# One replayed order for all engines behind attention in a retention, Mish and GLU kernel

## The chip, the cores and the metric

The kernel runs on one core of a Trainium2 chip. The metric is the device time of one execution in microseconds (us); lower is better. Engines are TensorE (PE; its weight loads are PEld), VectorE (DVE), ScalarE (ACT), GpSimd (POOL) and SyncE (SP), whose queue issues the transfers.

## The reference

Linear attention with a decaying state, then two feed-forward layers. Sizes: 2 batches, 8 heads, 768 positions, head width 64, so 1536 tokens by 512 features; inner widths 2048 and 1536; all float32.

```python
for t in range(S):
    state = gamma * state + outer(k[t], v[t])
    y[t] = scale * q[t] @ state
x = y as [1536, 512]
h = x @ moe_w_in                       # 512 x 2048
x = (h * tanh(softplus(h))) @ moe_w_out
gate = sigmoid(x @ moe2_w_gate)        # 512 x 1536
out = (gate * (x @ moe2_w_val)) @ moe2_w_out
```

## The kernel before, in words

**Precision.** Each float32 operand is kept as a rounded part (hi) and a remainder (lo). A product is three matmuls, hi·hi, hi·lo and lo·hi (mm3). So each weight and each activation needs a copy on ScalarE (hi) and a subtraction on DVE or GpSimd (lo); this pair is split, lines 94 to 96.

**Weights** come as 68 pieces of 512 KB. SP loads a piece into one of two staging buffers (raw), ScalarE and DVE decode it in two steps each (lines 106 to 109), and put (lines 192 to 200) writes hi and lo into a ring: 7 buffers "w", 4 "o", 2 "q". The kernel looks ahead: after each step of products, pump plans and emits the next weight as far as a ring has room.

**Products.** The 1536 tokens are 3 chunks of 512. From the third pair of blocks of the inner width on (and in the second layer), seven products replace eight (a Strassen-Winograd form): chunks 1 and 2 make the main product (512 columns, banks "h"), and the two halves of chunk 0 the side product (256 columns, banks "hx"). This needs sums of the inputs: main_sums forms T1 to T4 from chunks 1 and 2, side_sums the same (tiles ty, YT, and T4 in a part of xc) from the halves of chunk 0; sums (lines 202 to 211) does it for the weights on GpSimd. out1 and out2 are the second products of the two layers; each bank "o" is evicted into acc by ScalarE (first time, lines 467 and 481) or added by DVE (lines 469 and 483).

**Order.** While attention runs (the flag early is set), all five engines are bound to the written order through InOrder. The side sums are written into attention's blocks, two steps per block. Behind attention only TensorE keeps the written order; the framework's own scheduler orders the other engines at build time from its timeline simulation, within a priority for the second main sums (line 712). Every engine still runs its queue strictly in that fixed order on the chip. Which engine forms a remainder is written out: blocks and main sums on DVE, side sums and remainders of g on GpSimd, of weights on DVE and, from line 698 on, on GpSimd.

Of the kernel before, what the change touches and what calls it, by code (L numbers as in the profile page):

```python
# [9 lines left out]
F32 = mybir.dt.float32  # L10
F32R = mybir.dt.float32r
# [12 lines left out]
def kernel(ctx, tc, qk, nv, w1i, w1o, w2g, w2v, w2o, ma_in, og_in, sg_in, ck_in, out):  # L24
# [26 lines left out]
    AHEAD = 4  # L51

    early = [True]

    class InOrder:


        def __init__(self, engine):
            self.engine, self.last = engine, None

        def __getattr__(self, name):
            call = getattr(self.engine, name)
            if not early and self.engine is not nc.tensor:
                return call

            def ordered(**kw):
                with tc.issue_after(self.last) if self.last else nullcontext():
                    i = call(**kw)  # L68
                self.last = i.ins
                return i  # L70

            return ordered

    pe, dve, act, pool, sync = [InOrder(e) for e in (nc.tensor, nc.vector, nc.scalar, nc.gpsimd, nc.sync)]
    const = ctx.enter_context(tc.tile_pool(name="const", bufs=1))
    big = ctx.enter_context(tc.tile_pool(name="big", bufs=1))
    rings = {r: ctx.enter_context(tc.tile_pool(name="ring_" + r, bufs=RINGS[r])) for r in "wo"}
    upv = ctx.enter_context(tc.tile_pool(name="upv", bufs=3))
    stg = ctx.enter_context(tc.tile_pool(name="stg", bufs=STG))
    dec = ctx.enter_context(tc.tile_pool(name="dec", bufs=3))  # L80
    gp = ctx.enter_context(tc.tile_pool(name="gp", bufs=8))
    ep = ctx.enter_context(tc.tile_pool(name="ep", bufs=3))
    ps_h = ctx.enter_context(tc.tile_pool(name="ps_h", bufs=4, space=PSUM))
    ps_o = ctx.enter_context(tc.tile_pool(name="ps_o", bufs=2, space=PSUM))

    one_t = const.tile([P, 1], F32, name="one")
    sig = const.tile([P, 1], F32, name="sig")
# [53 lines left out]
    lo_eng = {"w": dve, "g": pool}  # L141

    def load_piece():
        n = cnt["dma"]
# [57 lines left out]
    def sums(key):  # L202
        v1, v2 = vs.pop(key)
        s = lo_eng["dcs"].tile([P, 4, H], F32, tag="s", name="s")
        a11, a12, a21, a22 = v1[:, :H], v1[:, H:], v2[:, :H], v2[:, H:]
        tt = pool.tensor_tensor
        tt(out=s[:, 0], in0=a21, in1=a22, op=ALU.add)
        tt(out=s[:, 1], in0=s[:, 0], in1=a11, op=ALU.subtract)
        tt(out=s[:, 2], in0=a11, in1=a21, op=ALU.subtract)
        tt(out=s[:, 3], in0=a12, in1=s[:, 1], op=ALU.subtract)  # L210
        sums_t[key] = s
# [56 lines left out]

    def put_plain():
        for kk in range(KK):  # L270
            split(acc_t[0][:, kk], xc_t[:, kk, 0], xc_t[:, kk, 1], dve)

    def put_block(n, c, k0, eng=None):
        for k in range(2):
            split(acc_t[c][:, k0 + k], b_t[n][:, k, 0], b_t[n][:, k, 1], eng or dve)

    def put_sums(x0, x1, bt, cols, eng):

        def new(n):
            return (up if cols == N else upv).tile([P, cols], F32, tag="u", name=n)  # L280

        sub = eng.tensor_tensor
        ts = []
        for k in range(2):
            t1, t2 = new("t1"), new("t2")
            sub(out=t1, in0=x1[:, k], in1=x0[:, k], op=ALU.subtract)
            split(t1, bt["T1"][:, k, 0], bt["T1"][:, k, 1], eng)
            sub(out=t2, in0=x1[:, 2 + k], in1=t1, op=ALU.subtract)
            split(t2, bt["T2"][:, k, 0], bt["T2"][:, k, 1], eng)
            sub(out=t2, in0=x0[:, 2 + k], in1=t2, op=ALU.subtract)  # L290
            ts.append(t2)
            sub(out=t1, in0=x1[:, 2 + k], in1=x1[:, k], op=ALU.subtract)
            split(t1, bt["T3"][:, k, 0], bt["T3"][:, k, 1], eng)
        return ts

    def put_t4(ts, bt, eng):
        for k in range(2):
            split(ts[k], bt["T4"][:, k, 0], bt["T4"][:, k, 1], eng)

    def main_sums():  # L300
        return put_sums(acc_t[1], acc_t[2], b_t, N, dve)

    def side_sums():

        x0, x1 = acc_t[0][:, :, :H], acc_t[0][:, :, H:]
        t = {}

        def form(n, k, in0, in1, to=None):
            if to is None:
                to = upv.tile([P, H], F32, tag="u", name="ty")  # L310
            pool.tensor_tensor(out=to, in0=in0, in1=in1, op=ALU.subtract)  # L311
            t[n, k] = to
            if n != "T4":
                low(n, k)

        def low(n, k):
            split(t[n, k], y_t[n][:, k, 0], y_t[n][:, k, 1], pool)

        steps = []
        for k in range(2):  # L320
            steps += [lambda k=k: form("T1", k, x1[:, k], x0[:, k]),
                      lambda k=k: form("T2", k, x1[:, 2 + k], t["T1", k]),
                      lambda k=k: form("T4", k, x0[:, 2 + k], t["T2", k], t["T2", k]),
                      lambda k=k: form("T3", k, x1[:, 2 + k], x1[:, k], t["T1", k])]
        return steps + [lambda k=k: low("T4", k) for k in range(2)]


    g_t = {}
# [159 lines left out]
    def seq(ss):  # L488

        def step(f):  # L490
            f()
            if not early:
                pump()

        return [lambda f=f: step(f) for f in ss]

# [55 lines left out]
    with ExitStack() as actx:  # L552
# [82 lines left out]
            at_state(j)  # L635
            at_out(j)

        ys = side_sums()

        def blocks(j0, dense, made):  # L640

            for j in range(j0, j0 + SPC):
                if j + 1 < NSUB:
                    at_scores(j + 1)
                if j >= SPC - 1:
                    pump()
                fin(j)
                flush_hi()
                at_prep(j + 2)
                load(j + AHEAD)  # L650
                load_piece()
                if j == j0 + SPC - 1:
                    flush()
                    made()
                if dense:
                    dense.pop(0)()
                if j >= SPC + 1:
                    run(ys[:2])
                    del ys[:2]
            run(dense)  # L660

        for t, table in ((ck, ck_in), (ma, ma_in), (og0, og_in), (sg, sg_in)):
# [12 lines left out]
        at_scores(0)  # L675
        blocks(0, [], put_plain)
        blocks(SPC, plain1(0) + plain1(1), lambda: (put_block("B11", 1, 0), put_block("B21", 1, 2)))
        blocks(2 * SPC, plain1(0, 1) + plain1(1, 1), early.clear)

    big2 = ctx.enter_context(tc.tile_pool(name="big2", bufs=1))  # L680
    up = ctx.enter_context(tc.tile_pool(name="up", bufs=3))
    dcs = ctx.enter_context(tc.tile_pool(name="dcs", bufs=1))
    rings["q"] = ctx.enter_context(tc.tile_pool(name="ring_q", bufs=RINGS["q"]))
    ps_x = ctx.enter_context(tc.tile_pool(name="ps_x", bufs=1, space=PSUM))
    hx["pool"], hx["own"] = ps_x, (0, 1)
    lo_eng["dcs"] = dcs
# [12 lines left out]
    L1 = FF1 // 2 - 1  # L699
    rest = out1(0, 2, G0)  # L700
    for i in range(I0, L1 + 1):
# [14 lines left out]
    run(ys[:8], plain2(1), ys[8:])  # L716
# [69 lines left out]
```

## Time and profile before

| | |
|---|---|
| median of 3 runs | 630.2 us (628.78 to 632.59) |
| profiled execution, its time | 630.01 us |
| its span | 628.2 us |
| TensorE, DVE, GpSimd, ScalarE busy | 591.5, 409.1, 346.5, 291.3 us |
| mean granted TensorE clock | 0.978 of full |

Attention takes roughly the first 82 us of the span, the first layer lies between 82 and 338, the second behind that. Times in rows are counted from the span's start. A matmul's record is longer than the step from one start to the next, because products overlap in the engine; 512-column products follow each other at some 0.23 us.

### The profile page before, as it was taken

What the parts mean: (1) busy time and instruction counts of PE and PEld (TensorE: products, weight loads), DVE (VectorE), ACT (ScalarE), POOL (GpSimd) and SP (SyncE); (2) the same over time, 40 slices, a digit from 0 to 9 for tenths busy, and PEclk for the clock granted to TensorE, in tenths of its full rate; (3) what the DMA queues carried; (4) which work ended last, traced back from release to release, by engine and by line L of the source; (5) the groups of instructions that cost most, each with busy time, mean ns of one, the idle gap of its engine ahead of it and who ended that gap; (6) DMA issues with size and microseconds to landing.
All of it is one profiled execution on the core that took longest, in us unless ns stands there. A gap on an engine that the chain in (4) does not pass through costs nothing.

```text
span 628.2 us, 8737 instructions
## 1 busy us (share of the span) xinstructions
PE 591.5 (94%) x3342; PEld 492.6 (78%) x3342; DVE 409.1 (65%) x585; ACT 291.3 (46%) x533; POOL 346.5 (55%) x299
## 2 busy tenths in 40 slices
PE   8987969799899999999979998989999999999997
PEld 7875858688688888888847777868888888888886
DVE  3875879606757575756798576538668767754564
ACT  1445575527436353536665575534534544440220
POOL 4476743308948484529893698637746745751200
PEclk9989898899899999999999999989999999999999
DMA  9962233202303131303130042203104104000004
GB/s 348 379 231 106 70 99 100 67 1 83 119 35 100 34 100 35 101 0 102 64 105 1 1 134 72 96 2 127 42 34 134 38 31 135 1 1 0 1 22 179
DMA packets 15593, 52.30 MB, mean 83 GB/s; under 512 B 1984, under 2 KB 2112, under 8 KB 15552
## 3 DMA queue, kind: packets, MB, share of 16 engines
q1 hardware_dynamic: 14976, 51.39, 23.4%
q8 instruction: 26, 0.43, 0.3%
q10 hardware_dynamic: 576, 0.36, 0.2%
q14 instruction: 15, 0.12, 0.1%
HBM read 48.60 MB, written 3.15 MB: 82 GB/s over the span
## 4 chain that ended last, share of the span: by engine, by line
PE 60%; DVE 14%; POOL 10%; ACT 7%; DMA 6%; issue 3%; SPq 0%; DVEq 0%; ACTq 0%; POOLq 0%
PE o L68 28%; PE h L68 20%; PE hx L68 11%; DVE v L109 3%; DMA raw<-w1i 2%; POOL ww L198 2%; DVE T L96 2%; POOL g L96 2%; DVE v L68 1%; DMA raw<-w2v 1%; DVE raw L108 1%; DVE raw L68 1%; DMA qk_t<-qk 1%; POOL ty L311 1%; POOL g L68 1%
## 5 line engine op out<-in xcount | busy, mean ns | idle before, releaser
L68 PE MATMUL o<-g,wo 128*128 128x512 f32 x576 | 147.3, 405 | 17.3 <-ACT acc L467 7.3
L96 POOL TENSOR_TENSOR g<-e,g 128x512 fp32r<-128x512 f32 x74 | 105.2, 1427 | 79.8 <-ACT g L95 75.3
L68 PEld LDWEIGHTS o<-g,wo 128*128 128x128 f32 x576 | 109.0, 195 | 44.1 <-ACT acc L467 8.2
L68 PE MATMUL o<-wo,g 128*128 128x512 f32 x432 | 110.0, 395 | 0.3 <-POOL g L96 0.3
L68 PE MATMUL h<-B,ww 128*128 128x512 f32 x372 | 95.6, 394 | 0.0
L68 PE MATMUL h<-T,ww 128*128 128x512 f32 x360 | 91.9, 392 | 2.7 <-DVE e L454 1.0
L68 PEld LDWEIGHTS o<-wo,g 128*128 128x128 f32 x432 | 78.7, 190 | 15.3 <-POOL g L96 0.7
L198 POOL TENSOR_TENSOR ww<-s,ww 128x512 fp32r<-128x512 f32 x32 | 43.1, 1352 | 80.3 <-ACT ww L197 74.9
L68 PEld LDWEIGHTS h<-T,ww 128*128 128x128 f32 x360 | 67.4, 189 | 17.9 <-DVE e L454 1.5
L68 PEld LDWEIGHTS h<-B,ww 128*128 128x128 f32 x372 | 69.6, 190 | 15.0 <-issue 0.5
L106 ACT ACTIVATE raw<-raw 128x512 int32<-128x512 uint8 x59 | 39.7, 672 | 86.6 <-DMA raw<-w1o 18.7
L108 DVE SCALAR_TENSOR_TENSOR raw<-raw 128x512 int32<-128x512 int32 x59 | 56.0, 948 | 34.3 <-ACT raw L106 33.8
L469 DVE TENSOR_TENSOR acc<-o,acc 128x512 f32<-128x512 f32 x72 | 48.8, 686 | 32.3 <-PE o L68 32.3
L109 DVE SCALAR_TENSOR_TENSOR v<-v,raw 128x512 int32<-128x512 int32 x59 | 60.9, 1032 | 13.9 <-ACT v L107 12.8
L483 DVE TENSOR_TENSOR acc<-o,acc 128x512 f32<-128x512 f32 x60 | 41.3, 688 | 31.0 <-PE o L68 30.9
L95 ACT ACTIVATE g<-e 128x512 fp32r<-128x512 f32 x77 | 48.4, 628 | 16.6 <-DVE e L454 16.0
L68 PE MATMUL hx<-xc,ww 128*128 128x256 f32 (+1 forms) x336 | 54.1, 299 | 0.3 <-DVE xc L68 0.3
L68 PEld LDWEIGHTS hx<-xc,ww 128*128 128x128 f32 x336 | 48.8, 190 | 5.2 <-DVE xc L68 0.7
L68 PEld LDWEIGHTS hx<-YT,ww 128*128 128x128 f32 x288 | 40.7, 190 | 8.6 <-DVE u L363 5.0
L68 PE MATMUL hx<-YT,ww 128*128 128x256 f32 x288 | 42.4, 283 | 3.8 <-DVE u L363 3.8
L198 POOL TENSOR_TENSOR wo<-v,wo 128x512 fp32r<-128x512 f32 x24 | 33.4, 1395 | 22.5 <-ACT wo L197 22.5
L107 ACT ACTIVATE v<-raw 128x512 f32<-128x512 f32 x59 | 39.4, 668 | 12.6 <-POOL s L210 5.7
(106 smaller groups left out, 786.9 us busy)
## 6 DMA issues: line engine op xcount, KB each, us to landing
raw<-w1i SPq DMA_DIRECT2D x16, 512.0 KB, 3.3
raw<-w1o SPq DMA_DIRECT2D x16, 512.0 KB, 3.3
qk_t<-qk SPq DMA_DIRECT2D x12, 512.0 KB, 6.0
nv_t<-nv SPq DMA_DIRECT2D x12, 512.0 KB, 6.9
raw<-w2g SPq DMA_DIRECT2D x12, 512.0 KB, 3.4
raw<-w2v SPq DMA_DIRECT2D x12, 512.0 KB, 3.3
raw<-w2o SPq DMA_DIRECT2D x12, 512.0 KB, 3.3
out<-acc SPq DMA_DIRECT2D x12, 256.0 KB, 2.0
```

The lines of the kernel that those rows point to most:

```text
L68: i = call(**kw)
L95: act.activation(out=hi, in_=raw, func=AF.Copy)
L96: eng.tensor_tensor(out=lo, in0=raw, in1=hi.bitcast(F32), op=ALU.subtract)
L106: act.activation(out=low, in_=rest, func=AF.Copy, scale=1.0 / 32, bias=-15.5 / 32)
L107: act.activation(out=v, in_=high.bitcast(F32), func=AF.Copy, scale=2.0 ** -112)
L108: dve.scalar_tensor_tensor(out=low, in0=high, scalar=SIGN, in1=low, op0=ALU.bitwise_and, op1=ALU.bitwise_or)
L109: dve.scalar_tensor_tensor(out=b, in0=b, scalar=3, in1=low, op0=ALU.logical_shift_left, op1=ALU.bitwise_or)
L198: late_lo.append(lambda: lo_eng["w"].tensor_tensor(out=lo, in0=v, in1=hi.bitcast(F32), op=ALU.subtract))
L311: pool.tensor_tensor(out=to, in0=in0, in1=in1, op=ALU.subtract)
L469: dve.tensor_tensor(out=acc, in0=o, in1=acc, op=ALU.add)
L483: dve.tensor_tensor(out=acc, in0=o, in1=acc, op=ALU.add)
```

## The change

Attention itself is written as before, in order, but the side sums are no longer in its blocks, and the flag early is cleared after attention's last products. From there on no call issues an instruction. Each call makes a Node with its engine (or two: "either" means GpSimd or DVE), its price, and the nodes that it must follow, from the words of the tiles that it reads and writes and from the buffers that it reuses. TensorE's nodes form a chain in written order. At the end replay() gives every node a rank, the price of the longest chain from it to the end, plays all nodes through on a clock, and issues them in the order of their planned starts, each behind the one before it on its engine. A free engine takes the ready node with the highest rank, but not one that would keep a single-engine node of higher rank waiting past its latest start. DVE takes an "either" node only if GpSimd could not start it by its latest start.

"Either" are now: remainders of weights, of g and of blocks, the steps of main and side sums, and the sums of weights. The steps of main and side sums are cut the same way (sums_of). pump is called with 12 instead of 1 (while recording), the priority of line 712 and the late assignments to DVE or GpSimd go.

```diff
-    pe, dve, act, pool, sync = [InOrder(e) for e in (nc.tensor, nc.vector, nc.scalar, nc.gpsimd, nc.sync)]
+    class Node:
+        def __init__(self, queues, name, kw):
...
+            self.cost = [q.cost(big.at.size, kw) for q in queues]
+            self.uses = [(v.home, k == "out", v.words()) for k, v in parts]
...
+            for home, writes, words in self.uses:
+                for n, w, m in home.uses:
+                    if (w or writes) and m & words:
+                        self.after.add(n)
...
+    pe = Queue(nc.tensor, lambda n, kw: (kw["rhs"].at.size + 32) / 2400, 0.2)
+    dve = Queue(nc.vector, lambda n, kw: (0.157 + 0.00104 * n) * (1 if psum(kw) else 1.3), 0.1)
+    act = Queue(nc.scalar, lambda n, kw: 0.17 + 0.0009 * min(n, N), 0.1)
+    pool = Queue(nc.gpsimd, lambda n, kw: 0.08 + 0.00258 * n, 0.1)
+    sync = Queue(nc.sync, lambda n, kw: 3.3 if isinstance(kw["out"], Part) else 1.6, 0.3)
+    either = Either(pool, dve)
...
+        for n in order:
+            n.rank = n.cost[0] + max((lag(n, m) + m.rank for m in n.then), default=0)
+        whole = max(n.rank for n in nodes)
...
+                for n in sorted((n for n in line[q] if n.ready <= now), key=lambda n: -n.rank):
+                    cost = n.cost[n.queues.index(q)]
+                    if len(n.queues) > 1 and q is dve:
+                        if max(now, free[pool]) + n.cost[0] <= whole + late - n.rank + n.cost[0]:
+                            continue
+                    end = now + cost
+                    if any(u.rank > n.rank and u.ready < end and end > max(u.ready, whole + late - u.rank)
+                           and u.ready > now and len(u.queues) == 1 for u in line[q]):
+                        continue
+                    pick = n
+                    break
...
+                late = max(late, n.start - (whole - n.rank)) if q is pe else late
...
+        for n in sorted(nodes, key=lambda n: (n.start, n.at)):
+            n.queue.issue(n.name, n.kw)
...
-        tt = pool.tensor_tensor
+        tt = either.tensor_tensor
...
-                pump()
+                pump(12)
...
-        ys = side_sums()
-
         def blocks(j0, dense, made):
...
-                if j >= SPC + 1:
-                    run(ys[:2])
-                    del ys[:2]
...
-        blocks(2 * SPC, plain1(0, 1) + plain1(1, 1), early.clear)
+        blocks(2 * SPC, plain1(0, 1) + plain1(1, 1), lambda: None)
+        flush()
+    early.clear()
...
+    lo_eng.update(dcs=Pool(name="dcs", bufs=1), w=either, g=either, x=either)
...
-    run(out1(0, 0, G0))
+    run(side_sums(), out1(0, 0, G0))
     ts = main_sums()
-    run(plain1(0, 2), plain1(1, 2))
+    run(ts[:6], plain1(0, 2), plain1(1, 2))
     b_t["T4"] = big2.tile([P, 2, 2, N], F32R, tag="T4", name="T4")
-    run(out1(0, 1, G0))
-    put_t4(ts, b_t, dve)
-    lo_eng["w"] = pool
+    run(ts[6:], out1(0, 1, G0))
...
-    with tc.high_priority():
-        put_t4(main_sums(), b_t, dve)
-        put_block("B22", 2, 2)
+    run(main_sums())
+    put_block("B22", 2, 2)
...
-            lo_eng["g"] = dve
             n = 3
...
+    replay()
```

## Rows read from the trace of the kernel before

**Rows 1.** The page's first part: busy us, share of the span, count.
```profile
PE 591.5 (94%) x3342; PEld 492.6 (78%) x3342; DVE 409.1 (65%) x585; ACT 291.3 (46%) x533; POOL 346.5 (55%) x299
```
**Rows 2.** Busy time by stage: stretch, its length, engines, clock, DMA share, GB/s.
```profile
24.00:82.00 58.00, 51.26 (x498) 40.92 (x497) 40.74 (x51) 27.47 (x54) 35.82 (x34) 0.91 0.45 163
82.00:121.00 39.00, 30.68 (x121) 24.12 (x120) 36.91 (x45) 27.73 (x53) 18.61 (x15) 0.91 0.30 95
121.00:142.00 21.00, 20.89 (x90) 17.30 (x91) 1.18 (x2) 4.52 (x9) 0.93 (x1) 0.92 0.00 1
142.00:163.00 21.00, 18.00 (x87) 14.67 (x86) 12.40 (x17) 17.04 (x32) 18.61 (x15) 0.93 0.31 101
163.00:313.00 150.00, 150.00 (x759) 127.94 (x758) 99.48 (x146) 73.28 (x133) 94.37 (x79) 1.00 0.19 64
313.00:386.00 73.00, 64.10 (x276) 49.33 (x275) 58.35 (x79) 44.05 (x79) 55.41 (x46) 1.00 0.21 71
386.00:420.00 34.00, 30.93 (x156) 26.10 (x155) 13.95 (x24) 14.94 (x28) 16.79 (x17) 0.95 0.14 47
420.00:604.00 184.00, 183.29 (x968) 157.42 (x967) 120.88 (x188) 74.03 (x135) 94.63 (x82) 1.00 0.14 46
```
**Rows 3.** The same view of the windows in which the granted clock was low.
```profile
44.00:47.40 3.40, 3.40 (x32) 2.76 (x28) 3.18 (x5) 1.74 (x3) 2.41 (x3) 0.50 0.41 154
61.00:67.90 6.90, 5.08 (x49) 4.46 (x50) 5.49 (x6) 3.46 (x7) 5.10 (x5) 0.51 0.21 76
91.80:98.60 6.80, 5.69 (x13) 4.46 (x14) 6.80 (x11) 4.28 (x10) 1.66 (x2) 0.50 0.01 2
122.50:125.90 3.40, 3.40 (x10) 2.63 (x9) 0.00 (x0) 0.40 (x1) 0.00 (x0) 0.50 0.00 0
```
**Rows 4.** TensorE's waits: us in total, times, the longest.
```profile
PE st L68 <- POOL YT L68: 5.6, 2, 3.6
PE o L68 <- POOL g L96: 4.5, 4, 2.4
PE o L68 <- DVE acc L469: 4.5, 5, 1.4
```
**Rows 5.** GpSimd in order of time in attention: start, us, instruction, idle before.
```profile
58.23 0.72 POOL L68 TENSOR_TENSOR ty<-acc 128x256 f32<-128x256 f32 x1
...
62.10 1.49 POOL L68 TENSOR_TENSOR vp<-nv_t,ck 128x512 f32<-128x512 f32 x1
```
**Rows 6.** The side sums' steps in attention by tile: count, ns min/median/max, first and last start.
```profile
L68 POOL TENSOR_TENSOR YT<-ty,YT x6: 722/730/743, 40.0 to 69.4; 128x256 fp32r<-128x256 f32 x6
L68 POOL TENSOR_TENSOR ty<-acc x4: 722/736/739, 38.7 to 68.2; 128x256 f32<-128x256 f32 x4
L68 POOL TENSOR_TENSOR ty<-acc,ty x4: 722/726/740, 40.7 to 67.5; 128x256 f32<-128x256 f32 x4
...
L68 POOL TENSOR_TENSOR xc<-ty,xc x2: 1177/1219/1261, 75.6 to 76.8; 128x256 fp32r<-128x256 f32 x2
```
**Rows 7.** ScalarE in order of time before 122.
```profile
119.40 0.66 ACT L106 ACTIVATE raw<-raw 128x512 int32<-128x512 uint8 x1 [2.22 <-DMA raw<-w1o]
...
120.49 1.06 ACT L467 ACTIVATE acc<-o 128x512 f32<-128x512 f32 x2
```
**Rows 8.** DVE in order of time before TensorE's start at 411.5.
```profile
410.40 0.69 DVE L108 SCALAR_TENSOR_TENSOR raw<-raw 128x512 int32<-128x512 int32 x1 [1.59 <-ACT raw L106]
411.01 0.41 DVE L363 TENSOR_TENSOR u<-hx,s 128x256 f32<-128x256 f32 x1
```
**Rows 9.** Remainders: tile T on DVE (82 to 121), then GpSimd in order of time.
```profile
L96 DVE TENSOR_TENSOR T<-t,T x8: 677/680/1782, 94.9 to 117.2; 128x512 fp32r<-128x512 f32 x8
...
153.20 1.31 POOL L198 TENSOR_TENSOR ww<-s,ww 128x512 fp32r<-128x512 f32 x1
154.46 1.74 POOL L96 TENSOR_TENSOR g<-e,g 128x512 fp32r<-128x512 f32 x1
```
**Rows 10.** The chain that ended last, its longest piece: start, us, what.
```profile
603.67 20.61 PE o L68 x90
```

More of the change, by code (lines that the diff above doesn't have):

```diff
@@ L53 @@
     early = [True]
-    class InOrder:
-        def __init__(self, engine):
-            self.engine, self.last = engine, None
-        def __getattr__(self, name):
[L62 to L72, printed above, removed]
@@ L74 @@
-    pe, dve, act, pool, sync = [InOrder(e) for e in (nc.tensor, nc.vector, nc.scalar, nc.gpsimd, nc.sync)]
-    const = ctx.enter_context(tc.tile_pool(name="const", bufs=1))
[L76 to L84, printed above, removed]
+    WIDTH = {F32: 4, F32R: 4, I32: 4, I64: 8, U8: 1}
+    nodes = []
+    class Home:
+        def __init__(self, make, before, psum):
+            self.make, self.before, self.psum = make, before, psum
+            self.real, self.uses = make() if early else None, []
@@ new lines, with __init__, __getitem__, bitcast @@
+    class Part:
+        def __init__(self, home, at, width, ops):
+            self.home, self.at, self.width, self.ops = home, at, width, ops
+        def __getitem__(self, key):
+            return Part(self.home, self.at[key[1:]], self.width, self.ops + (lambda t: t[key],))
+        def bitcast(self, dtype):
+            w = WIDTH[dtype]
+            at = (self.at[..., None] + np.arange(self.width // w) * w).reshape(*self.at.shape[:-1], -1)
+            return Part(self.home, at, w, self.ops + (lambda t: t.bitcast(dtype),))
+        def rearrange(self, form, **kw):
+            at = self.at.reshape(-1, kw["t"]) if kw else self.at.reshape(-1)
+            return Part(self.home, at, self.width, self.ops + (lambda t: t.rearrange(form, **kw),))
+        def words(self):
+            m = np.zeros((1 + int(self.at.max()) // 4 + 1), bool)
+            m[self.at.ravel() // 4] = True
+            if self.width == 8:
+                m[self.at.ravel() // 4 + 1] = True
+            return int.from_bytes(np.packbits(m, bitorder="little").tobytes(), "little")
+        def real(self):
+            if self.home.real is None:
+                self.home.real = self.home.make()
+            t = self.home.real
+            for f in self.ops:
+                t = f(t)
+            return t
@@ new lines, with __init__, tile @@
+    class Pool:
+        def __init__(self, bufs, **kw):
+            self.pool, self.bufs, self.psum = ctx.enter_context(tc.tile_pool(bufs=bufs, **kw)), bufs, "space" in kw
+            self.made = {}
+        def tile(self, shape, dtype, name, tag=None):
+            made = self.made.setdefault(tag or name, [])
+            kw = {"tag": tag} if tag else {}
+            before = made[-self.bufs] if len(made) >= self.bufs else None
+            made.append(Home(lambda: self.pool.tile(shape, dtype, name=name, **kw), before, self.psum))
+            at = np.arange(int(np.prod(shape[1:]))).reshape(shape[1:]) * WIDTH[dtype]
+            return Part(made[-1], at, WIDTH[dtype], ())
@@ new lines @@
+    class Node:
+        def __init__(self, queues, name, kw):
+            self.queues, self.name, self.kw = queues, name, kw
+            parts = [(k, v) for k, v in kw.items() if isinstance(v, Part)]
+            big = max((v for _, v in parts), key=lambda v: v.at.size)
+            self.cost = [q.cost(big.at.size, kw) for q in queues]
+            self.uses = [(v.home, k == "out", v.words()) for k, v in parts]
+            if name == "matmul" and not kw["start"]:
+                self.uses.append((kw["out"].home, False, self.uses[0][2]))
+            self.after, self.then = set(), []
+            for home, writes, words in self.uses:
+                for n, w, m in home.uses:
+                    if (w or writes) and m & words:
+                        self.after.add(n)
+            for home, writes, words in self.uses:
+                home.uses.append((self, writes, words))
+            self.at = len(nodes)
+            nodes.append(self)
@@ new lines, with __init__, issue @@
+    class Queue:
+        def __init__(self, engine, cost, lag):
+            self.engine, self.cost, self.lag, self.last = engine, cost, lag, None
+        def issue(self, name, kw):
+            call = getattr(self.engine, name)
+            kw = {k: v.real() if isinstance(v, Part) else v for k, v in kw.items()}
+            with tc.issue_after(self.last) if self.last else nullcontext():
+                i = call(**kw)
+            self.last = i.ins
+        def __getattr__(self, name):
+            return lambda **kw: self.issue(name, kw) if early else Node([self], name, kw)
@@ new lines, with __init__, __getattr__, psum @@
+    class Either:
+        def __init__(self, *queues):
+            self.queues = queues
+        def __getattr__(self, name):
+            return lambda **kw: Node(list(self.queues), name, kw)
+    def psum(kw):
+        return any(isinstance(v, Part) and v.home.psum for v in kw.values())
+    pe = Queue(nc.tensor, lambda n, kw: (kw["rhs"].at.size + 32) / 2400, 0.2)
+    dve = Queue(nc.vector, lambda n, kw: (0.157 + 0.00104 * n) * (1 if psum(kw) else 1.3), 0.1)
+    act = Queue(nc.scalar, lambda n, kw: 0.17 + 0.0009 * min(n, N), 0.1)
@@ new lines, with replay, lag, enter @@
+    pool = Queue(nc.gpsimd, lambda n, kw: 0.08 + 0.00258 * n, 0.1)
+    sync = Queue(nc.sync, lambda n, kw: 3.3 if isinstance(kw["out"], Part) else 1.6, 0.3)
+    either = Either(pool, dve)
+    def replay():
+        chain = [n for n in nodes if n.queues[0] is pe]
+        for n in nodes:
+            for home, _, _ in n.uses:
+                if home.before:
+                    n.after |= {m for m, _, _ in home.before.uses}
+        for m, n in zip(chain, chain[1:]):
+            n.after.add(m)
+        for n in nodes:
+            n.after.discard(n)
+            for m in n.after:
+                m.then.append(n)
+        open_ = {n: len(n.then) for n in nodes}
+        todo, order = [n for n in nodes if not n.then], []
+        while todo:
+            n = todo.pop()
+            order.append(n)
+            for m in n.after:
+                open_[m] -= 1
+                if not open_[m]:
+                    todo.append(m)
+        assert len(order) == len(nodes), len(order)
+        def lag(m, n):
+            return 0 if m.queues[0] is n.queues[0] else m.queues[0].lag
+        for n in order:
+            n.rank = n.cost[0] + max((lag(n, m) + m.rank for m in n.then), default=0)
+        whole = max(n.rank for n in nodes)
+        late = 0
+        free = {q: 0.0 for q in (pe, dve, act, pool, sync)}
+        wait = {n: len(n.after) for n in nodes}
+        line = {q: [] for q in free}
+        done = []
+        def enter(n):
+            n.ready = max((m.end + lag(m, n) for m in n.after), default=0.0)
+            for q in n.queues:
+                line[q].append(n)
+        for n in nodes:
+            if not wait[n]:
+                enter(n)
+        now = 0.0
+        while len(done) < len(nodes):
+            moved = False
+            for q in free:
+                if free[q] > now or not line[q]:
+                    continue
+                pick = None
+                for n in sorted((n for n in line[q] if n.ready <= now), key=lambda n: -n.rank):
[6 more added lines that the diff above has]
+                           and u.ready > now and len(u.queues) == 1 for u in line[q]):
+                        continue
+                    pick = n
+                    break
+                if not pick:
+                    continue
+                n = pick
+                n.start, n.end, n.queue = now, now + n.cost[n.queues.index(q)], q
+                free[q] = n.end
+                late = max(late, n.start - (whole - n.rank)) if q is pe else late
+                for k in n.queues:
+                    line[k].remove(n)
+                done.append(n)
+                moved = True
+                for m in n.then:
+                    wait[m] -= 1
+                    if not wait[m]:
+                        enter(m)
+            if not moved:
+                later = [t for t in free.values() if t > now] + [n.ready for q in free for n in line[q] if n.ready > now]
+                now = min(later)
+        for n in sorted(nodes, key=lambda n: (n.start, n.at)):
+            n.queue.issue(n.name, n.kw)
@@ L86 @@
+    const = ctx.enter_context(tc.tile_pool(name="const", bufs=1))
+    big = Pool(name="big", bufs=1)
+    rings = {r: Pool(name="ring_" + r, bufs=RINGS[r]) for r in "wo"}
+    upv = Pool(name="upv", bufs=3)
+    stg = Pool(name="stg", bufs=STG)
+    dec = Pool(name="dec", bufs=3)
+    gp = Pool(name="gp", bufs=8)
+    ep = Pool(name="ep", bufs=3)
+    ps_h = Pool(name="ps_h", bufs=4, space=PSUM)
+    ps_o = Pool(name="ps_o", bufs=2, space=PSUM)
     one_t = const.tile([P, 1], F32, name="one")
@@ L140 @@
     steps, late_hi, late_lo, sums_t, vs = [], [], [], {}, {}
-    lo_eng = {"w": dve, "g": pool}
+    lo_eng = {"w": dve, "g": pool, "x": dve}
     def load_piece():
@@ L270, in put_plain, with put_block @@
         for kk in range(KK):
-            split(acc_t[0][:, kk], xc_t[:, kk, 0], xc_t[:, kk, 1], dve)
-    def put_block(n, c, k0, eng=None):
+            split(acc_t[0][:, kk], xc_t[:, kk, 0], xc_t[:, kk, 1], lo_eng["x"])
+    def put_block(n, c, k0):
         for k in range(2):
[L275 to L306, printed above, removed]
+            split(acc_t[c][:, k0 + k], b_t[n][:, k, 0], b_t[n][:, k, 1], lo_eng["x"])
+    def sums_of(x0, x1, bt, cols, eng):
+        t, low = {}, []
         def form(n, k, in0, in1, to=None):
             if to is None:
-                to = upv.tile([P, H], F32, tag="u", name="ty")
-            pool.tensor_tensor(out=to, in0=in0, in1=in1, op=ALU.subtract)
+                to = (up if cols == N else upv).tile([P, cols], F32, tag="u", name="t")
+            eng.tensor_tensor(out=to, in0=in0, in1=in1, op=ALU.subtract)
+            hi, lo = bt[n][:, k, 0], bt[n][:, k, 1]
+            act.activation(out=hi, in_=to, func=AF.Copy)
+            while low:
+                low.pop()()
+            low.append(lambda: eng.tensor_tensor(out=lo, in0=to, in1=hi.bitcast(F32), op=ALU.subtract))
@@ L312, in form @@
             t[n, k] = to
[L313 to L317, printed above, removed]
         steps = []
@@ L322, in side_sums, with main_sums @@
                       lambda k=k: form("T2", k, x1[:, 2 + k], t["T1", k]),
-                      lambda k=k: form("T4", k, x0[:, 2 + k], t["T2", k], t["T2", k]),
                       lambda k=k: form("T3", k, x1[:, 2 + k], x1[:, k], t["T1", k])]
-        return steps + [lambda k=k: low("T4", k) for k in range(2)]
+        for k in range(2):
+            steps.append(lambda k=k: form("T4", k, x0[:, 2 + k], t["T2", k], t["T2", k]))
+        return steps + [lambda: low.pop()()]
+    def main_sums():
+        return sums_of(acc_t[1], acc_t[2], b_t, N, either)
+    def side_sums():
+        return sums_of(acc_t[0][:, :, :H], acc_t[0][:, :, H:], y_t, H, pool if early else either)
     g_t = {}
@@ L677 @@
         blocks(SPC, plain1(0) + plain1(1), lambda: (put_block("B11", 1, 0), put_block("B21", 1, 2)))
-        blocks(2 * SPC, plain1(0, 1) + plain1(1, 1), early.clear)
[L680 to L686, printed above, removed]
+        blocks(2 * SPC, plain1(0, 1) + plain1(1, 1), lambda: None)
+        flush()
+    early.clear()
+    big2 = Pool(name="big2", bufs=1)
+    up = Pool(name="up", bufs=3)
+    rings["q"] = Pool(name="ring_q", bufs=RINGS["q"])
+    hx["pool"], hx["own"] = Pool(name="ps_x", bufs=1, space=PSUM), (0, 1)
+    lo_eng.update(dcs=Pool(name="dcs", bufs=1), w=either, g=either, x=either)
     for n in ("T4", "B22", "T1", "T2", "T3"):
@@ L711 @@
     run(out1(L1, 2), plain2(0))
-    with tc.high_priority():
-        put_t4(main_sums(), b_t, dve)
-        put_block("B22", 2, 2)
+    run(main_sums())
+    put_block("B22", 2, 2)
     ys = side_sums()
-    run(ys[:8], plain2(1), ys[8:])
+    run(ys[:6], plain2(1), ys[6:])
     weave(seq(main_steps((2, 0), glu_of(0), True)), out2(0, 0))
```

## The prediction

> **What bounds the kernel now.** I read the totals first [rows 1]: TensorE is busy for 591.5 of 628.2 us, no other engine for more than 409, so time can only come out of the 36.7 us in which TensorE is idle and out of stretches in which it runs slowly. The second view is the busy time by stage [rows 2]. The reader is to see two kinds of stage. In 163-313, 420-604 and up to the last product (604 onwards), TensorE hardly stops: 150.00 of 150, 183.29 of 184, and at the end 90 products in 20.61 us, 0.229 us each [rows 10]. Nothing an order can do makes these shorter. The others have holes: 24-82 (58.00 less 51.26 = 6.7 us), 82-121 (8.3), 121-142 (0.1), 142-163 (3.0), 313-386 (8.9), 386-420 (3.1). The third view is the granted clock [rows 3]: six windows at 0.50, which is the 1.2 GHz level, each behind a hole. A busy microsecond there does half a microsecond's work, so they cost half of their busy time: 1.7 (44.0), 2.5 (61.0), 2.8 (91.8), and 1.7 each for the three like the row at 122.5 (122.5, 160.0, 412.6).
>
> The fourth view, TensorE's waits and the queue behind them, says why the holes are there. Attention waits on GpSimd, 5.6 us in two waits [rows 4]: v' ("vp"), which the state product needs, stands behind four ty/YT steps of the side sums [rows 5]. The last hole before 121 is an order's fault: the eviction of the output bank (ACT acc, line 467) stands behind a decode that waits for a transfer until 119.40 [rows 7]. So is the hole before 411.5 (in 386-420): a DVE decode waits for ACT and for the transfer before it, and the small addition u that TensorE needs stands behind it [rows 8]. In 142-163 GpSimd works 18.61 of 21 us while DVE works 12.40 [rows 2]. In 82-121 DVE works 36.91 of 39 and in 313-386 both are loaded (DVE 58.35, GpSimd 55.41 of 73): there it is partly load, not only order.
>
> **The change, part by part**, against the profiled execution: 630.0 us (span 628.2 and 1.8 around it; the median of the three runs is 630.2).
>
> (1) The side sums leave attention: 16 GpSimd steps, 8 ty and 6 YT at about 0.73 us and 2 xc at 1.22 [rows 6], 12.7 us of GpSimd, and eight ScalarE copies between them. Attention keeps its written order. Without them vp starts at 58.3 instead of 62.10 and the state product follows the scores; what goes at most is 5.6 us of waits [rows 4] and 1.7 + 2.5 of slow clock [rows 3], 9.8 us. At least nothing goes, if ScalarE's decodes (late in the same blocks) or the addition behind them are as late. I take 7: the two waits are on vp alone, and nearly 3 us stay, because another GpSimd step precedes vp in each block and the clock may fall once all the same.
>
> (2) 82-163. Loss now: 8.3 + 0.1 + 3.0 idle and 2.8 + 1.7 + 1.7 slow, 17.6 us. The plan ranks each step by the work that depends on it, so an eviction that TensorE waits for goes ahead of a decode, and a decode is not put where its transfer (priced 3.3 us) has not landed. Against that stands the load that comes here: the 12.7 us of side sums. Their cover is the hole at 121-142, where GpSimd works 0.93 and DVE 1.18 of 21 us [rows 2]; without that cover they cost up to 12.7 us. Steps that were DVE's alone in the first stretch (4 block remainders, 16 main-sum steps) may now go to GpSimd, which was idle for half of it (18.61 of 39). Recovered: at most 17.6, at least 17.6 less 12.7 = 4.9. I take 12, the upper half, because the 21 us hole is larger than all that moves in.
>
> (3) 313-386. Loss 8.9 idle. Here 26 DVE steps (4 + 4 + 2 remainders, 16 main-sum steps) become free to go either way, and the 16 side steps can be put off until the side products of the second layer need them. But both engines are loaded. Recovered: at most 8.9; below zero, if GpSimd takes what DVE did faster: 26 steps at 0.63 (worked out under the second rival) are 16 lost. I take 5: 4.5 of the 8.9 us end on an eviction by DVE (DVE acc, line 469 [rows 4]), which the plan ranks first, and a little more on remainders.
>
> (4) 386-420: 3.1 idle and 1.7 slow, a pure order fault [rows 8]; between 0 and 4.8, I take 4.5, since the plan knows the transfer's time.
>
> (5) The dense stages, 163-313 and 420-604. Now 0.7 us idle [rows 2], so there is nothing to win. Every engine now follows a fixed order made with mean prices, and DVE helps with a remainder only when GpSimd would come too late, so a step that is slow once can hold TensorE. Between a gain of 0.7 and a loss of 20 (a hole like that at 411 with its slow clock in every fourth of the 16 rounds); I take a loss of 2, as rings and banks hold more than one round's work ahead.
>
> At no cost: pump(12) only records; TensorE's own products keep their written order; SP's loads keep their sequence, and the transfer engines are at most 0.31 busy behind attention in any stage before the outputs [rows 2], which is the cover. If the plan delays one, its decode is late, which is the hole of (4). The tail (one addition and one transfer behind the last product) stays.
>
> A row on the price of sharing: the remainder of T on DVE takes 0.68 us as a rule and up to 1.78 [rows 9], and GpSimd's steps take 1.31 or 1.74 [rows 9] according to what runs beside them. The plan prices DVE at 0.90 for such a step at all times and both engines as independent. The Trainium skill ("SBUF — State Buffer", section "Who interferes with whom") says that a DVE instruction with two SBUF inputs and a GpSimd instruction that reads SBUF exclude each other, and that the later one waits for the whole of the first. By that rule the trace agrees (0.68 + 1.10 of waiting is under one GpSimd step of 1.31), and steps (2) and (3) would be those of the second rival.
>
> **Sum:** -7 - 12 - 5 - 4.5 + 2 = -26.5, so 603.5 us.
>
> **Rivals.**
> First: both crowded stretches keep their loss, because it is load. For it: DVE at 36.91 of 39 and both engines near 80% in 313-386. Against it: the 21 us hole beside the first, and evictions that stood behind decodes. Only (1) and (4) remain: 630.0 - 7 - 4.5 = 618.5.
>
> Second, the other side: GpSimd and DVE work as one resource, and the plan hands GpSimd what DVE did faster. Place: the 46 steps of the two sum stretches that were DVE's (4 + 16 and 4 + 4 + 2 + 16). Price: 1.31 instead of 0.68 us of the common resource, 0.63 each [rows 9]. With (2) and (3) recovering nothing, 11.5 us of gain remain elsewhere; from 18 of the 46 steps on the kernel is slower than before. With all 46: 630.0 - 11.5 + 29 = 647.5. For it: in 82-121 DVE is near its limit already and GpSimd is preferred by the plan. Against it: the plan lets DVE take a step when GpSimd would be late, which is just when it hurts.
>
> Third: the orders come out much as they were, because the previous schedule was also fixed ahead and the product order doesn't change. Then (1) alone: 623. For it: 163-313 and 420-604 are perfect under the old orders. Against it: rows 7 and 8 show orders that a plan with a 3.3 us transfer would not make.
>
> **How the numbers follow.** Forecast 0.56, with a range of its own of 592 to 614; still better than that 0.06 (all of 9.8, 17.6, 8.9, 4.8 and 0.7 recovered would be 588.2). First rival 0.17, third 0.08, second 0.13. About 0.5%, 3 us, is what a measurement of this kernel tells from no change. Faster: 0.56 + 0.06 + 0.17 and half of the third rival, 0.83; the same: the other half and 0.02 of the second, 0.06; slower 0.11. The range runs from 590, near the floor, to 624: outside it lie the second rival, half of the third and a little below, 2 in 10 together.
>
> **What would show it.** (1) No TensorE wait on a side sum, and no half clock between 40 and 70; all that follows starts some 7 us earlier. (2) The waits on ACT acc are gone, and in the 40 us behind that start DVE and GpSimd are loaded alike, without a hole of 20 us. (3) Idle TensorE in the stretch that answers to 313-386 falls from 8.9 to about 4 us. (4) No half clock behind the change of layers. (5) The stages of 150 and 184 us stay as long as they are. The forecast is wrong if GpSimd's total goes well over 346.5 us [rows 1] with its mean step longer, and TensorE's waits on GpSimd's remainders (line 96) grow from now 4.5 us [rows 4]: that is the second rival; or if waits turn up in the dense stages.

## The result and the profile after

The changed kernel takes 592.55 us (592.18 to 592.68); the kernel before, with a fourth run, has a median of 629.49. The ratio is 0.9408, with a 95% interval of [0.9368, 0.9449]. The profiled execution took 592.18 us, its span 590.2. The page's first part answers to [rows 1]:

```profile
PE 577.4 (98%) x3342; PEld 484.3 (82%) x3342; DVE 385.5 (65%) x540; ACT 296.1 (50%) x533; POOL 399.0 (68%) x344
```

TensorE has 12.8 us of idle time left where it had 36.7. 45 steps went from DVE to GpSimd. The next view is the busy time by stage (columns as in [rows 2]); the stretches are cut at the same products as there, so that the lengths can be compared:

```profile
24.00:71.20 47.20, 46.91 (x498) 37.62 (x497) 43.14 (x54) 26.43 (x50) 24.53 (x19) 1.00 0.55 200
71.20:101.00 29.80, 27.57 (x122) 22.48 (x121) 7.68 (x7) 19.45 (x38) 27.77 (x26) 1.00 0.16 54
101.00:120.10 19.10, 19.10 (x91) 16.02 (x90) 5.03 (x4) 9.12 (x16) 18.94 (x17) 1.00 0.00 1
120.10:137.60 17.50, 16.23 (x87) 13.67 (x86) 10.79 (x16) 12.17 (x23) 17.42 (x17) 1.00 0.29 91
137.60:287.40 149.80, 149.80 (x759) 127.81 (x758) 108.89 (x155) 86.01 (x153) 106.35 (x89) 1.00 0.25 81
287.40:353.30 65.90, 63.42 (x276) 49.30 (x275) 42.72 (x53) 36.81 (x68) 65.31 (x55) 1.00 0.15 48
353.30:383.50 30.20, 29.36 (x156) 25.00 (x155) 21.20 (x28) 20.53 (x38) 27.72 (x26) 1.00 0.30 95
383.50:566.00 182.50, 182.50 (x967) 157.34 (x966) 121.82 (x190) 77.33 (x138) 97.16 (x85) 1.00 0.16 51
```

The reader is to see that the clock is 1.00 in every stage, that the stages which were dense keep their length, and that GpSimd is now the full engine in the crowded ones (27.77 of 29.80, 65.31 of 65.90) while DVE is idle for most of the first. The lengths fell by 10.8 us in attention (58.0 to 47.2), 14.6 in the three stretches behind it (39 + 21 + 21 to 29.8 + 19.1 + 17.5), 0.2, 7.1, 3.8 and 1.5: 38.0 us, the whole difference of the spans. What waits are left, against [rows 4]:

```profile
PE o L143 <- ACT acc L143: 2.7, 2, 2.2
PE hx L143 <- DVE u L143: 2.4, 2, 1.3
PE warm L143 <- DVE z L143: 1.2, 1, 1.2
PE hx L143 <- DVE hx L143: 0.8, 1, 0.8
```

The three waits that are left out are of 0.8 us and less. No wait on a side sum and none on a GpSimd remainder is among them.

### The profile page after: what moved, and what is told of

It reads as the page before. It is cut to its first block, busy times and chain, and to the rows that moved or that the text cites. A ratio compares the mean times of both kernels' runs of the same rounds, so it can differ in the third digit from the quotient of the medians.

```text
span 590.2 us, 8777 instructions
## 1 busy us (share of the span) xinstructions
PE 577.4 (98%) x3342; PEld 484.3 (82%) x3342; DVE 385.5 (65%) x540; ACT 296.1 (50%) x533; POOL 399.0 (68%) x344
## 4 chain that ended last, share of the span: by engine, by line
PE 78%; POOL 10%; DVE 4%; DMA 3%; ACT 3%; issue 2%; SPq 0%; DVEq 0%; POOLq 0%; ACTq 0%
PE o L143 32%; PE h L143 29%; PE hx L143 14%; POOL t L143 3%; PE ao L143 2%; POOL T L143 2%; DMA raw<-w1i 2%; PE sc L143 1%; POOL g L143 1%; DVE v L143 1%; POOL xc L143 1%; DMA qk_t<-qk 1%; POOL B L143 1%; DVE raw L143 1%; POOL s L143 1%
## 5 line engine op out<-in xcount | busy, mean ns | idle before, releaser
L143 POOL TENSOR_TENSOR g<-e,g 128x512 fp32r<-128x512 f32 x81 | 112.5, 1398 | 78.9 <-ACT g L143 74.2
L143 PE MATMUL o<-g,wo 128*128 128x512 f32 x576 | 140.0, 392 | 2.3 <-ACT acc L143 2.2
L143 PEld LDWEIGHTS o<-g,wo 128*128 128x128 f32 x576 | 105.4, 188 | 25.7 <-ACT acc L143 2.7
L143 POOL TENSOR_TENSOR ww<-s,ww 128x512 fp32r<-128x512 f32 x35 | 50.7, 1450 | 53.8 <-ACT ww L143 53.7
L143 DVE SCALAR_TENSOR_TENSOR raw<-raw 128x512 int32<-128x512 int32 x68 | 68.6, 1009 | 16.7 <-ACT raw L143 16.5
L143 DVE SCALAR_TENSOR_TENSOR v<-v,raw 128x512 int32<-128x512 int32 x68 | 71.1, 1046 | 6.4 <-ACT v L143 4.9
L143 ACT ACTIVATE raw<-raw 128x512 int32<-128x512 uint8 x68 | 45.5, 670 | 43.3 <-DMA raw<-w2g 13.8
L143 ACT ACTIVATE e<-h 128x512 f32<-128x512 f32 x57 | 33.9, 595 | 60.3 <-PE h L143 38.8
L143 ACT ACTIVATE v<-raw 128x512 f32<-128x512 f32 x68 | 45.0, 666 | 13.5 <-POOL s L143 10.2
L143 DVE TENSOR_TENSOR h<-h,u 128x512 f32<-128x512 f32 x54 | 37.5, 695 | 21.3 <-PE h L143 20.9
```

## The experiments

**Order or sharing.** My theory was that the order makes the gain behind attention (an eviction no longer stands behind a decode). Its rival was that sharing makes it. The changed kernel, with the engines written out as before:

```diff
-        tt = either.tensor_tensor
+        tt = pool.tensor_tensor
...
-        return sums_of(acc_t[1], acc_t[2], b_t, N, either)
+        return sums_of(acc_t[1], acc_t[2], b_t, N, dve)
...
-    lo_eng.update(dcs=Pool(name="dcs", bufs=1), w=either, g=either, x=either)
+    lo_eng.update(dcs=Pool(name="dcs", bufs=1), w=dve, g=pool, x=dve)
...
```

> The changed kernel with the engines of the kernel before written out again (blocks and main sums DVE; sums of weights, side sums and remainders of g GpSimd; remainders of weights DVE, from out1 of chunk 1 on GpSimd; the last g on DVE). Only the order is the plan's. If the order makes the gain behind attention: 592 to 598 us. If sharing between GpSimd and DVE makes it, the DVE-bound stretch behind attention (36.91 of 39 us) and the change of layers keep their holes of 8 us each: 605 to 612 us.

592.16 us (591.94 to 592.26), no slower than with sharing. Its page, and its stages, cut at the same products as those of the changed kernel above:

```profile
PE 576.9 (98%) x3342; PEld 485.7 (82%) x3342; DVE 417.6 (71%) x585; ACT 295.1 (50%) x533; POOL 345.4 (59%) x299
```
```profile
71.30:105.60 34.30, 29.31 (x121) 23.41 (x120) 31.07 (x29) 23.25 (x45) 29.12 (x25) 0.95 0.11 32
105.60:126.70 21.10, 19.55 (x90) 16.07 (x91) 12.40 (x17) 10.78 (x20) 5.17 (x5) 1.00 0.36 123
126.70:142.70 16.00, 16.00 (x87) 13.78 (x86) 7.77 (x13) 12.55 (x22) 12.84 (x12) 1.00 0.20 67
...
292.50:354.40 61.90, 61.12 (x276) 49.97 (x275) 54.26 (x72) 37.58 (x69) 47.59 (x42) 1.00 0.15 50
354.40:383.60 29.20, 29.20 (x156) 25.04 (x155) 20.11 (x28) 19.43 (x36) 23.48 (x22) 1.00 0.35 107
```

DVE and GpSimd do what they did before, 585 and 299 instructions, and the gain is whole: it is the order. Sharing moves time about, and its two sides cancel: the three stretches behind attention take 71.4 us here against 66.4 with sharing, the change of layers and the stretch behind it 61.9 and 29.2 against 65.9 and 30.2. So sharing won 5.0 us in the first place and lost 5.0 in the second.

**What in the plan makes the order.** First the price of a transfer, 3.3 us in the change:

```diff
-    sync = Queue(nc.sync, lambda n, kw: 3.3 if isinstance(kw["out"], Part) else 1.6, 0.3)
+    sync = Queue(nc.sync, lambda n, kw: 0.3, 0.3)
```

> The changed kernel with one number changed in the plan: a transfer is priced 0.3 us instead of 3.3. If the price of transfers is what keeps decodes from standing in front of evictions, holes like those before 121 and 411 return, 3 to 5 us each with their slow clock, in some of the 22 changes of weights: 600 to 615 us, TensorE waiting on ACT acc or DVE u behind ACT or DVE waits for raw. If pieces are loaded so early that their price plays no part: 592 to 594 us.

632.95 us (631.65 to 636.47), ratio to the kernel before 1.0072 [1.0044, 1.0099]: one number undoes the gain behind attention and more, worse than either theory expected. (The edit also prices the transfers of the result at 0.3 us, which were 1.6.) TensorE's three largest waits are on DVE, 28.6 us together, and one of those places, in order of time, shows the same picture as [rows 8], an addition behind a decode that came late:

```profile
PE hx L143 <- DVE hx L143: 11.9, 8, 3.8
PE o L143 <- DVE acc L143: 9.3, 10, 2.2
PE hx L143 <- DVE u L143: 7.4, 7, 2.6
```

```profile
410.17 0.65 ACT L143 ACTIVATE raw<-raw 128x512 int32<-128x512 uint8 x1 [4.38 <-DMA raw<-w2o]
...
410.86 0.69 DVE L143 SCALAR_TENSOR_TENSOR raw<-raw 128x512 int32<-128x512 int32 x1 [3.42 <-ACT raw L143]
411.46 0.43 DVE L143 TENSOR_TENSOR hx<-hx,u 128x256 f32<-128x256 f32 x1
...
411.94 1.55 PE L143 MATMUL hx<-xc,ww 128*128 128x256 f32 x6 [3.80 <-DVE hx L143]
```

Two further runs put 1.6 and 6.6 in the place of 3.3:

> The changed kernel with a transfer priced 1.6 us in the plan instead of 3.3 (0.3 gave 633 us). A piece takes 3.2 to 3.5 us to land by the profile. If what counts is whether the price lies under the true time, decodes still stand some 1.7 us too early and part of the loss is there: 600 to 620 us. If the loss at 0.3 came from a plan thrown over as a whole by near-free transfers: 592 to 596 us.

> The changed kernel with a transfer priced 6.6 us, twice the true time. If a price above the true time only leaves slack: 591 to 595 us, and ScalarE waits less for transfers than the 41.5 us in the changed kernel. If it makes weights late in the plan, so that other work is put in front of them: 598 to 610 us with TensorE waiting for weights.

602.63 us (600.59 to 604.36) and 593.07 us (592.78 to 594.26). The view of all waits gives ScalarE's waits for weights, of which the sum over the five kinds counts; at 0.3 us, and then all that is left at 6.6:

```profile
ACT raw L143 <- DMA raw<-w1o: 35.2, 11, 5.4
ACT raw L143 <- DMA raw<-w2o: 31.2, 11, 4.4
...
ACT raw L143 <- DMA raw<-w2v: 30.0, 10, 5.7
...
ACT raw L143 <- DMA raw<-w2g: 24.4, 10, 3.9
...
ACT raw L143 <- DMA raw<-w1i: 17.3, 7, 3.2
```
```profile
ACT raw L143 <- DMA raw<-w1i: 3.2, 1, 3.2
...
ACT raw L143 <- DMA raw<-w2o: 1.5, 1, 1.5
```

| price of a transfer in the plan | ScalarE waits for weights | time |
|---|---|---|
| 0.3 us | 138.1 us | 632.95 us |
| 1.6 us | 79.4 us | 602.63 us |
| 3.3 us (the change) | 41.5 us | 592.55 us |
| 6.6 us | 4.7 us | 593.07 us |
| kernel before | 84.4 us | 629.49 us |

The two sides are not alike: too low a price costs 10 and 40 us, double the true one (3.2 to 3.5 us to landing by the page) about half a microsecond. ScalarE's waits go with the price, but they alone don't set the time: the kernel before and the plan with 1.6 us have nearly the same sum and lie 27 us apart, of which attention makes 10.8.

Second, the rank. The plan takes the node written first:

```diff
-                for n in sorted((n for n in line[q] if n.ready <= now), key=lambda n: -n.rank):
+                for n in sorted((n for n in line[q] if n.ready <= now), key=lambda n: n.at):
```

> The changed kernel whose plan takes the ready node written first instead of the one of highest rank (the guard for higher ranks stays). If the rank makes the gain, evictions stand behind the up to 12 weights written in front of them and rings fill early: 605 to 640 us. If true prices make it and the written order is near the rank's: 592 to 600 us.

606.92 us (605.01 to 607.64), 14.4 more. TensorE's waits on ACT acc are 5.9 us in three waits, 2.7 in two with the rank, and a wait of 2.9 on DVE's u is new. TensorE's idle time grows by 6.5 us in all (19.3 against 12.8) and its busy time by 6.3 (583.7 against 577.4): the granted clock is at 0.50, for instance, from 81.6 to 86.7. So the rank carries about 14 us and a true transfer price up to 40; at a price of 0.3 us the rank alone did not save the plan. No run varies the number of weights that pump looks ahead (12), so its part in the gain is open.

**The side sums in attention.** The changed kernel with them put back:

```diff
+        ys = side_sums()
+
         def blocks(j0, dense, made):
...
+                if j >= SPC + 1:
+                    run(ys[:2])
+                    del ys[:2]
...
-    run(side_sums(), out1(0, 0, G0))
+    run(out1(0, 0, G0))
```

> The changed kernel with one edit undone: the side sums stand in attention's blocks again, on GpSimd, two steps a block. If the terms are separate, 592.5 + 10.8 = 603 us, with TensorE's waits on v' and the half clock between 40 and 70 back. If the replayed part gains from being rid of the 12.7 us of GpSimd (36.7 of 38.8 us busy behind attention now), its 3.5 us of idle TensorE there goes too and the time is 598 to 600 us.

601.46 us (600.96 to 603.94), 8.9 more, between the two. The wait is the predicted one, and GpSimd's queue in order of time shows it again, v' behind three steps of the sums:

```profile
PE st L143 <- POOL vp L143: 8.0, 4, 3.1
```
```profile
38.77 0.74 POOL L143 TENSOR_TENSOR t<-acc 128x256 f32<-128x256 f32 x1
39.59 0.74 POOL L143 TENSOR_TENSOR t<-acc,t 128x256 f32<-128x256 f32 x1
40.28 0.73 POOL L143 TENSOR_TENSOR YT<-t,YT 128x256 fp32r<-128x256 f32 x1
40.97 1.05 POOL L143 TENSOR_TENSOR vp<-nv_t,ck 128x512 f32<-128x512 f32 x1
```

Attention then ends 11.4 us later (out1 starts at 82.6 instead of 71.2) and 2.5 us come back behind it: TensorE's wait on ACT acc falls from 2.7 to 0.5.

The other way round, the kernel before with the sums moved and nothing else, was meant to show the same:

```diff
-        ys = side_sums()
-
...
-                if j >= SPC + 1:
-                    run(ys[:2])
-                    del ys[:2]
...
-    run(out1(0, 0, G0))
+    run(side_sums(), out1(0, 0, G0))
```

> The kernel before with one edit: the side sums leave attention's blocks and are written (on GpSimd) in front of the first out1; no replay, engines as written. If the terms of the sum are separate, attention ends near 71 as in the changed kernel (82 before), and GpSimd, idle for 20 of 39 us behind it, takes the 12.7 us: 618 to 622 us. If the moved load is what the replay had to absorb, the framework's order gives part of it back as new TensorE waits behind attention: 625 to 632 us, with attention's end near 71 all the same.

623.4 us (622.83 to 623.85), between the two ranges. Both stories missed, since attention ended at 77.1, not near 71. The framework, free to order these steps, put them back among attention's, earlier than they had been written:

```profile
29.45 3.00 POOL L96 TENSOR_TENSOR YT<-ty,YT 128x256 fp32r<-128x256 f32 x3
...
38.84 1.55 DVE L68 TENSOR_TENSOR ww<-v,ww 128x512 fp32r<-128x512 f32 x1 [0.99 <-ACT ww L68]
...
40.44 2.57 PE L68 MATMUL hx<-xc,ww 128*128 128x512 f32 x10 [0.85 <-DVE ww L68]
```

The decoded weight's remainder takes 1.55 us on DVE beside these steps, and TensorE waits 0.85 us for it. So this run does not price step (1) by itself; the run before it does.

**GpSimd's load and DVE's help.** Two kernels: "either" means GpSimd alone; and DVE helps 4 us earlier.

```diff
-    either = Either(pool, dve)
+    either = Either(pool)
```

> The changed kernel with 'either' meaning GpSimd alone: DVE helps with nothing. GpSimd is busy 36.7 of 38.8, 20.8 of 21 and 63.1 of 64 us in the crowded stretches of the changed kernel, and DVE takes some 17 steps there. If GpSimd's load binds there, those steps cost up to 1.3 us each: 600 to 615 us, with TensorE waiting on GpSimd remainders in the first 60 us behind attention and at the change of layers. If the order alone matters, whoever works: 592 to 596 us.

```diff
-                        if max(now, free[pool]) + n.cost[0] <= whole + late - n.rank + n.cost[0]:
+                        if max(now, free[pool]) + n.cost[0] <= whole + late - n.rank + n.cost[0] - 4.0:
```

> The changed kernel with DVE helping 4 us before GpSimd would be late, instead of at the last moment. If the help that comes at the last moment makes the small holes at 291 to 381 (about 6 us together): 586 to 590 us. If two-input steps on DVE then stand in front of the additions that TensorE waits for: 594 to 600 us.

599.28 us (597.66 to 599.71), just under the first range, and 592.27 us (592.08 to 593.05), between its two ranges. Without help, the change of layers grows: GpSimd is busy 69.32 of 70.6 us there, TensorE idle for 5.1, and the clock falls once. TensorE's waits on GpSimd's remainders are only 1.0 us of these; the longest is on ACT acc, an eviction that stood behind a copy of a side sum that waited for GpSimd.

```profile
287.40:358.00 70.60, 65.54 (x275) 50.24 (x275) 35.96 (x45) 37.61 (x68) 69.32 (x61) 0.98 0.11 37
```

The last-minute help is thus worth 6.7 us, for 11 steps (529 instructions of DVE against 540). Helping earlier neither gains nor loses: small holes go, and one wait of 2.7 us on a sigmoid (PE h on ACT e) comes. What put that one there I did not follow.

**The plan's start.** The plan counts every engine as free when it starts. In the changed kernel's trace they finish attention first, and the first eviction of out1 stands behind copies, two of which wait for GpSimd, and two decode steps. ScalarE in order of time:

```profile
74.86 0.42 ACT L143 ACTIVATE YT<-t 128x256 fp32r<-128x256 f32 x1 [1.06 <-POOL t L143]
...
77.04 0.65 ACT L143 ACTIVATE raw<-raw 128x512 int32<-128x512 uint8 x1
77.59 0.64 ACT L143 ACTIVATE v<-raw 128x512 f32<-128x512 f32 x1
78.42 0.60 ACT L143 ACTIVATE acc<-o 128x512 f32<-128x512 f32 x1 [0.19 <-POOL t L143]
```
```diff
-        free = {q: 0.0 for q in (pe, dve, act, pool, sync)}
+        free = {pe: 0.0, dve: 0.6, act: 1.5, pool: 2.9, sync: 0.0}
```

> The changed kernel with the engines' start in the plan taken from its trace (TensorE 0, DVE 0.6, ScalarE 1.5, GpSimd 2.9 us) instead of 0 for all. If the hole of 2.2 us at 77 to 79 comes from the plan's start, which counts the engines as free while they finish attention: 589 to 590.5 us and no wait on ACT acc there. If the hole is load: 592.5 us, or the hole moves by some us.

590.33 us (589.79 to 590.59), and out1's 48 products run without a hole. On top of that, the better assignment of each stretch: sharing up to out1 of chunk 1, the engines of the kernel before from there on (only the sums of weights and the side sums may still go either way).

```diff
...
+    lo_eng.update(w=pool, g=pool, x=dve)
...
-    run(main_sums())
+    run(main_sums(dve))
...
+            lo_eng["g"] = dve
```

> The kernel with the later start of the engines, and from out1 of chunk 1 on the engines of the kernel before (blocks and main sums DVE, remainders of weights and g and the side products' start as they were, the last g DVE); sums of weights and side sums stay free to go either way. If sharing helps only in the first stretch and costs at the change of layers (5 us of holes in 290 to 356, none of them in the run with the order alone): 583 to 588 us. If the holes there are due to something else than GpSimd's load: 590 to 593 us.

586.36 us (585.28 to 586.61), ratio to the kernel before 0.9301 [0.9274, 0.9328]: the fastest version, ahead of both kernels. Its stages, cut at the same products again:

```profile
71.40:135.80 64.40, 63.02 (x296) 52.09 (x295) 27.57 (x28) 41.00 (x77) 62.23 (x55) 1.00 0.15 50
135.80:286.30 150.50, 150.06 (x759) 127.70 (x758) 112.69 (x155) 86.11 (x153) 107.80 (x90) 1.00 0.25 81
286.30:348.50 62.20, 61.38 (x276) 49.96 (x275) 52.74 (x72) 37.23 (x68) 45.31 (x42) 1.00 0.16 51
348.50:377.90 29.40, 29.40 (x157) 25.07 (x156) 20.16 (x28) 19.38 (x36) 23.72 (x22) 1.00 0.33 107
377.90:560.50 182.60, 182.60 (x967) 157.39 (x966) 121.66 (x191) 77.19 (x138) 96.05 (x83) 1.00 0.15 50
```

The change of layers and the stretch behind it took 65.9 and 30.3 us in the run without the fixed assignment; they are where the 4 us come from. 2.6 us of idle TensorE are left between 71 and 560.

## Why the prediction was right, and where it was not

The direction and the reason were right: the order, made with a true transfer price, takes the holes away. The size was less well known: 592.55 us is 11 us under the forecast of 603.5 and only 0.55 inside the forecast's own range of 592 to 614, so that it still lies there is partly luck. The steps:

(1) 7 forecast, 10.8 measured in attention's length, 8.9 when undone (attention 11.4 longer, 2.5 back behind it). The mechanism was right (v' behind the sums, [rows 5]). The size was not: even my upper bound of 9.8 fell short. It held the two waits on GpSimd and the clock; the wait of 0.9 us on DVE for a block's remainder went too, and I had expected some slow clock to stay, of which none did.

(2) 12 forecast, 14.6 measured. The moved load found its cover, as predicted: GpSimd works 18.94 of 19.10 us where it had worked 0.93 of 21 [rows 2]. Two of the signs named for it did not come: 2.7 us of waits on ACT acc are left, and DVE and GpSimd are not loaded alike behind attention (12.7 and 46.7 of 48.9 us).

(3) 5 forecast, 7.1 measured. (4) 4.5 forecast, 3.8 measured: 0.8 us are idle there still, a wait on DVE's hx.

(5) A loss of 2 forecast, 1.7 gained (0.2 and 1.5), above the bound of 0.7 too. This step failed in sign: I feared that a fixed order made with mean prices would hold TensorE in the dense stages. It held it nowhere in 332 us. With the transfer price wrong it does: 164.91 of 180 us busy in 120 to 300 of that run. What held TensorE there was a price that is too low, not the fixed order as such.

The terms missed by 3.8 + 2.6 + 2.1 - 0.7 + 3.7 = 11.5 us, nearly all to one side: 38.0 us of span against a sum of 26.5.

First rival, load keeps its holes: fallen. The run with the order alone has the same engines and steps as before, and keeps the gain. Second rival: half of it came. GpSimd did get what DVE did faster (399.0 us busy, up 52.5), and was full where the rival put it. Behind attention this still won time, since GpSimd had idle time there, and DVE took what would have been late. Its price shows at the change of layers: taking those steps back gives 4.0 us (590.33 to 586.36), not 16. So the 7.1 us of (3) are what the order won less what sharing lost. Third rival, the orders hardly differ: fallen. A planned order is not good by itself, though: with the price of 0.3 us it lands at the old time although attention is 10.8 us shorter in it.

What the prediction takes as the basis of the second rival, that a two-input step of DVE and a step of GpSimd exclude each other, can be read in the changed kernel's trace. One place in order of time:

```profile
22.12 1.04 POOL L143 TENSOR_TENSOR vp<-nv_t,ck 128x512 f32<-128x512 f32 x1 [1.79 <-DMA nv_t<-nv]
22.39 1.32 DVE L143 TENSOR_TENSOR ww<-v,ww 128x512 fp32r<-128x512 f32 x1
...
23.12 1.49 POOL L143 TENSOR_TENSOR og<-og,sg 128x512 f32<-128x512 f32 x1
```

DVE's step ends 0.55 us behind GpSimd's first, and GpSimd's second 0.90 us behind DVE's. All 17 subtractions of DVE with both inputs in SBUF and 512 columns that start while a GpSimd step runs end 0.55 to 0.62 us behind that step, however early they started; the 11 GpSimd steps of 512 columns that start while one of DVE's runs end 0.90 to 1.17 us behind it. So whichever comes later waits for the earlier one, as the prediction said; the rival built on it was outweighed.

## What to carry to other kernels

Where every queue is in order, look for what a hole's last wait stood behind: an eviction behind a decode behind a transfer is a fault of the order, and here it went without any work changing its engine. A planner needs true prices above all where an engine would sit on a wait; price a transfer at or above its measured time, as here double the time cost half a microsecond and half of it 10 us. Judge sharing between engines by stretch, cut at the same products: it won 5 us in one stretch here and lost as much in another, which the time of the whole does not show.

## What I had not expected of the hardware

GpSimd ran at 65.31 of 65.90 us, and DVE beside it at 42.72, with TensorE idle for only 2.5. Against the kernel before, the 45 steps that changed engines cost GpSimd 52.5 us (1.17 each) and saved DVE 23.6 (0.52 each); against the run with the order alone, which is the fairer comparison, 53.6 (1.19) and 32.1 (0.71). The exchange is bad in sum, and yet it won time where the taker had been idle. The granted clock stayed at 1.00 through a hole of 2.2 us in the changed kernel; in the run with the order alone it fell behind a hole of 3.7 us at 77 to 81 (0.95 in that stage). But the length of one hole does not decide it: the kernel before has the clock at 0.50 from 44.0 on [rows 3] behind a hole of 2.0 us (5.6 less 3.6, [rows 4]), and in the run without DVE's help it fell near 334, behind holes of 0.6, 0.8 and 1.9 us between 327 and 333.
